# Attention feature map and MoE on one Trainium2 core: another staging of the MoE weights, issued by ScalarE, and other landing tiles for keys and queries

## The chip, the core and the metric

The kernel runs as one program on one core of a Trainium2 chip. The metric is the device time of one execution in microseconds (us). The kernel before was timed in three runs: 1204.83, 1207.55 and 1209.04 us, with the median at 1207.55 us. A fourth execution was recorded by the hardware profiler; all rows quoted here come from that one. The engines are called PE (matrix multiply), PEld (its weight loads), DVE (vector), ACT (scalar), POOL (GpSimd) and SP (the engine that here only issues DMAs).

## What is computed

Eight batches of eight heads with 576 tokens of 64 values go through an attention with a feature map, and the result through a two-layer MLP with 512, 2048 and 512 columns.

```python
def phi(x):
    proj = np.einsum('bhsd,df->bhsf', x, w_phi)
    proj = proj - np.max(np.abs(proj), axis=-1, keepdims=True)
    return np.concatenate([np.exp(proj), np.exp(-proj)], axis=-1)
q_p, k_p = phi(q), phi(k)
kv = np.einsum('bhsf,bhsd->bhfd', k_p, v)
z = np.sum(k_p, axis=2)
out = einsum('bhsf,bhfd->bhsd', q_p, kv) / (einsum('bhsf,bhf->bhs', q_p, z)[..., None] + 1e-06)
x = out as (4608 tokens, 512)
h = x @ w_in
return np.maximum(0.01 * h, h) @ w_out
```

The two weight matrices lie in HBM as 64-bit floats. The kernel brings each 128x512 piece of them in as 128x1024 32-bit words and rebuilds a 32-bit value from the halves of each pair on ACT and DVE. Then it splits that value into a high and a low part (names ending in h and l), because a matmul of the fast 32-bit type is taken three times: high by high, high by low, low by high.

## The kernel before: work, order and names

**Attention.** Two heads make a pair, so there are 32 pairs i, four to a batch. For each pair a key phase (`k_phase`) projects the keys (PE lines L405 or L244), takes the absolute maximum and the exponentials, and sums them against the values into one PSUM tile "c" (L224), which has a single buffer. A query phase (`q_phase`) projects the queries (L342 for pairs 4 to 7, L344 and L345 from pair 8 on). DVE transposes the result into the tile tq and reduces it (L346, L348). Three small DMAs gather the maxima over partitions (L350) and three spread them again (L355). Then DVE subtracts and transposes (L361, L363), ACT takes exponentials (L368, L369), DVE makes the high part (L375), and PE multiplies with the key sums (L384, L386, L389). Pairs 0 to 3 (batch 0) have versions of their own, the "first" phases (L405, L440, L517), which run with everything in tiles called f1 to f4. Pairs 0 to 7 use plain 32-bit matmuls, which show twice each in the profile.

**MLP.** Tokens go in 18 blocks of 256. A step (block, ft) has a first layer of 12 matmuls with 256 columns (L571, L572, L574), the activation (L578), the split, and a second layer of 6 matmuls with 512 columns (L591 to L593). Blocks 0 and 1 advance together through the 16 slices ft, and this is when the weights are staged; from block 2 on each block runs through all ft. The output of batch b stands in half b % 2 of the tile `ring` ("the x words"), and a block can only be split into xh and xl when the attention of all its tokens is there. Block 2 needs batch 1 (pairs 4 to 7), block 4 needs batch 2 (pairs 8 to 11), block 6 needs batch 3 (pairs 12 to 15).

**Weight staging** (`load_weights`). There are 32 pieces n = 0 to 31, the input weight and the output weight of each ft in turn. Each is a load (L169), an absolute value on ACT (L174), three DVE operations (L175 to L177), a second ACT operation (L179), a DVE addition (L180), a copy on ACT and a difference on DVE. The landing places before:

```python
if n < 10:    raw = two halves of ring[:, 1]
elif n < 24:  raw = (f4[:, 0:1024], f4[:, 1024:2048], f1[:, 0:1024])[n % 3]
else:         raw = qs tile if n % 2 else ring[:, 1, 2:4]
```

**What sets the order.** The program gives every operation a priority (front first, then attention, then staging, then the MLP), and a list scheduler with a cost model puts the instructions of each engine into one fixed order when the kernel is built. On the chip each engine runs its list in that order and waits at each instruction for what it needs. SP's list holds all DMAs before: loads of keys, values, queries and weights, the small DMAs of the query phase, and the output.

**Landing tiles before.** `load_k` (L191) lands the keys of pairs 5 and 7 in the tile `ks` and all others in `rk`; one buffer each. The values go into `rv` (L192 to L194), the queries into `rq` (L200). The third part of batch 0's queries (`first_load_q`, L470) also lands in `rq`.

Of the kernel before, what the change touches and what calls it, by code (L numbers as in the profile page):

```python
# [9 lines left out]
F32 = mybir.dt.float32  # L10
F32R = mybir.dt.float32r
I32 = mybir.dt.int32
U32 = mybir.dt.uint32
AF = mybir.ActivationFunctionType
# [30 lines left out]
def attention_moe_kernel(ctx: ExitStack, tc: tile.TileContext, q, k, v, vt, w_phi, w_in, w_out, out):  # L45
# [5 lines left out]
    def ct(shape, dt, name):  # L51
        return cp.tile(shape, dt, tag=name, name=name)

    def st(shape, dt, tag):
        return sp.tile(shape, dt, tag=tag, name=tag, bufs=BUFS.get(tag, 1))

    cnt = {}

# [5 lines left out]
    def copy_(key, o, i):  # L64
        e = pick(key) or "a"
        if e == "a":
            nc.scalar.copy(o, i)  # L67
        else:
            (nc.vector if e == "v" else nc.gpsimd).tensor_copy(o, i)  # L69

    def tt_(key, o, a, b, op):
        (nc.vector if pick(key) == "v" else nc.gpsimd).tensor_tensor(o, a, b, op=op)  # L72
# [8 lines left out]
    def weight(which, part, ft):  # L81
        g, f = divmod(ft, 4)
        if (which, part, g) not in weights:
            name = f"w{which}{part}{g}"
            weights[which, part, g] = (cp.tile([P, 4, DM], F32R, tag="late", name=name, bufs=4) if g == 3 else
                                       ct([P, 4, DM], F32R, name))
        return weights[which, part, g][:, f]
# [65 lines left out]
            nc.scalar.copy(wq_h[r], w)  # L153
            nc.vector.tensor_tensor(wq_l[r], w, wq_h[r].bitcast(F32), op=ALU.subtract)

    tail_stage = ring[:, 1, 2:4].rearrange("p a s -> p (a s)")

    def load_weights():
        n = 0
        for ft in range(NFT):  # L160
            for which, src in ((0, w_in), (1, w_out)):
                if n < 10:
                    raw = ring[:, 1, 2 * (n % 2) : 2 * (n % 2) + 2].rearrange("p a s -> p (a s)")[:, 0:1024]
                elif n < 24:
                    raw = (f4[:, 0:1024], f4[:, 1024:2048], f1[:, 0:1024])[n % 3]
                else:
                    raw = st([P, 2 * S], F32, "qs")[:, 0:1024] if n % 2 else tail_stage[:, 0:1024]
                raw = raw.bitcast(I32)
                nc.sync.dma_start(raw, src[:, ft].bitcast(I32))  # L169
                raw = raw.rearrange("p (n t) -> p n t", t=2)  # L170
                low, top = raw[:, :, 0], raw[:, :, 1]
                w = st([P, DM], F32, "ql")
                wi = w.bitcast(I32)
                nc.scalar.activation(w, top.bitcast(F32), AF.Abs)  # L174
                nc.vector.tensor_scalar(w, w, TINY, HUGE, op0=ALU.max, op1=ALU.min)  # L175
                nc.vector.tensor_scalar(wi, wi, 3, 0x3FFFFFF8, op0=ALU.logical_shift_left, op1=ALU.bitwise_and)
                nc.vector.scalar_tensor_tensor(wi, top, -0x40000000, wi, op0=ALU.bitwise_and, op1=ALU.bitwise_or)  # L177
                cr = st([P, DM], I32, "kvl")
                nc.scalar.activation(cr, low.bitcast(U32), AF.Copy, scale=2.0 ** -29)  # L179
                nc.vector.tensor_tensor(wi, wi, cr, op=ALU.add)  # L180
                h, l = weight(which, "h", ft), weight(which, "l", ft)
                copy_("h", h, w)
                tt_("l", l, w, h.bitcast(F32), ALU.subtract)
                n += 1

    kraw, qraw = {}, {}

    def load_k(i):
        rk = st([P, S], F32, "ks" if i < NK and i % 2 else "rk")
        rv = st([P, 10, 66], F32, "rv")  # L190
        nc.sync.dma_start(rk, k[i])  # L191
        nc.sync.dma_start(rv[:, 0:8, 0:64], v[i])  # L192
        nc.sync.dma_start(rv[0:64, 8:10, 0:64], vt[i])
        nc.sync.dma_start(rv[64:128, 8:10, 0:64], vt[i])  # L194
        nc.gpsimd.memset(rv[:, :, 64:66], 1.0)
        kraw[i] = rk, rv

    def load_q(i):
        rq = st([P, S], F32, "rq")
# [4 lines left out]

    def k_phase(i):
        nat = i < NK
        rk, rv = kraw.pop(i)
        if not nat:
            ks = st([P, 2, S], F32R, "ks")
            for j in range(2):  # L210
# [4 lines left out]
            copy_("vh", vh[:, :, 0:64], rv[:, :, 0:64])  # L215
            for r, c in ((slice(0, P), slice(0, 8)), (slice(64, P), slice(8, 10))):
                tt_("vl", vl[r, c], rv[r, c, 0:64], vh[r, c, 0:64].bitcast(F32), ALU.subtract)
        if i + 1 < B * NP:
            load_k(i + 1)
        yield  # L220
        kvp = pt("c")

# [4 lines left out]
        for g in range(3):  # L227
# [28 lines left out]
                nc.vector.tensor_scalar(m4n[r, 0 : 2 * w], m4[r, 0 : 2 * w], -1.0, None, op0=ALU.mult)  # L256
            if nat:
                nc.vector.tensor_tensor(pmk[r, 0 : 2 * w], pkv, mb, op=ALU.subtract)
            yield
            for s in range(w):  # L260
                c = 2 * g + s
# [24 lines left out]
                else:  # L286
# [3 lines left out]
                    for j in range(2):  # L290
                        kv_mm(j, vl[:, 8 + j], kst[:, j])
                        kv_mm(j, vh[:, 8 + j], kst[:, j], last=True)
                yield
        kvs = st([P, 2, 256], F32, "ek").rearrange("p a (b f) -> p a b f", b=2)[0:66]
        copy_("kvs", kvs, kvp[0:66].rearrange("p (a b f) -> p a b f", a=2, b=2))
        yield
# [114 lines left out]
    def first_k_phase(i):  # L411
        od = i % 2
        rk, rv = first_k.pop(i)
        if i == 2:
            load_k(NP)
        yield
        kvp = pt("h")
        for g in range(3):
# [43 lines left out]
    def first_load_q(u):  # L462
        t0, w = units[u]
        if u == 0:
            rq = st([P, NP, w], F32, "ks")
        elif u == 1:
            rq = part(f2, 0, [NP, w])
        else:
            rq = st([P, NP, w], F32, "rq")
        nc.sync.dma_start(rq, q[0:NP, :, t0 : t0 + w].rearrange("a p t -> p a t"))  # L470
        first_q[u] = rq

# [215 lines left out]
```

## Time and profile before

| | |
|---|---|
| median of three runs | 1207.55 us (1204.83 to 1209.04) |
| the profiled execution | 1207.22 us, of which the span of the trace is 1205.4 us |
| PE busy in the span | 1168.8 us, 97% |
| DVE, ACT, POOL busy | 747.7, 861.8, 631.5 us |
| matmul records | 7496 |
| weight loads of 512 KB | 28 in rows of ring and f tiles, 4 more in qs |

A row of the timeline gives start, duration, engine, line, operation, output and inputs, count, and in brackets the idle time before it with what ended it. A row of the windows gives a stretch, its length, and then the busy time and (number of instructions) of PE, PEld, DVE, ACT and POOL, the clock granted to PE as a share, the busy share of the DMA engines and GB/s. Ends of matmuls are modelled and overlap, so that the distance between starts is what a matmul costs. Lines are those of the kernel before unless said otherwise.

### The profile page before, as it was taken

To read this page: it belongs to the slowest core of one execution; us is meant where nothing else is said; L and a number is where in the kernel's file an instruction comes from. 1 tells how busy PE (TensorE), PEld (TensorE's weight loads), DVE (VectorE), ACT (ScalarE), POOL (GpSimd) and SP (SyncE) were. 2 spreads that over 40 slices of the span, in tenths; PEclk is the share of its full clock that TensorE was granted. 3 is DMA by queue.
4 is the path that set the end of the run, shared out by engine and by line. 5 is a ranking of instruction groups with operands and counts; after the bars stand their busy time and mean duration, and the time that the engine had idled before them with its cause. 6 is when DMAs were issued, how large, how long until landed. Compare 5 with 4: busy or idle time off the path is not lost.

```text
span 1205.4 us, 21633 instructions
## 1 busy us (share of the span) xinstructions
PE 1168.8 (97%) x7496; PEld 1035.9 (86%) x7496; DVE 747.7 (62%) x1327; ACT 861.8 (71%) x2267; POOL 631.5 (52%) x709
## 2 busy tenths in 40 slices
PE   8899999899998999899999999999999999999998
PEld 5577778699997999799998999899989999989997
DVE  5979984566767675766677666767876767510000
ACT  5977875778787787777787877778777788543232
POOL 0042222456566676666666666656566766453232
PEclk9999999899998999899999999999999999999999
DMA  7425241201111011111111011111011110000000
GB/s 215 142 81 167 88 116 32 77 23 33 50 32 48 18 44 33 50 24 32 50 32 40 22 50 33 40 33 50 21 40 32 41 33 19 3 18 5 14 18 18
DMA packets 70846, 57.82 MB, mean 48 GB/s; under 512 B 53201, under 2 KB 54353, under 8 KB 70737
## 3 DMA queue, kind: packets, MB, share of 16 engines
q1 hardware_dynamic: 70736, 56.44, 16.6%
q8 instruction: 59, 0.97, 0.3%
q14 instruction: 51, 0.41, 0.1%
HBM read 46.20 MB, written 9.44 MB: 46 GB/s over the span
## 4 chain that ended last, share of the span: by engine, by line
PE 69%; DVE 10%; ACT 9%; issue 4%; DMA 4%; SPq 2%; POOL 2%; DVEq 0%; POOLq 0%; ACTq 0%
PE h L571 9%; PE h L574 9%; PE h L572 9%; PE acc L591 8%; PE acc L592 8%; PE acc L593 8%; PE c L224 5%; PE a L384 2%; DMA mx<-mx 2%; PE a L244 2%; PE a L389 2%; PE a L386 2%; DMA m<-m 2%; DVE tq L361 1%; SPq L350 1%
## 5 line engine op out<-in xcount | busy, mean ns | idle before, releaser
L72 POOL TENSOR_TENSOR gl<-g,gh 128x256 fp32r<-128x256 f32 x288 | 231.3, 806 | 327.9 <-ACT gh L67 259.9
L571 PE MATMUL h<-xh,w0h 128*128 128x256 f32 x1088 | 281.1, 285 | 4.4 <-ACT g L578 2.4
L572 PE MATMUL h<-xh,w0l 128*128 128x256 f32 x1088 | 277.5, 282 | 0.0
L571 PEld LDWEIGHTS h<-xh,w0h 128*128 128x128 f32 x1088 | 205.9, 189 | 18.3 <-ACT g L578 4.2
L591 PE MATMUL acc<-w1h,gh 128*128 128x512 f32 x544 | 215.3, 396 | 0.7 <-DVE o L69 0.4
L592 PE MATMUL acc<-w1l,gh 128*128 128x512 f32 x544 | 214.8, 395 | 0.0
L572 PEld LDWEIGHTS h<-xh,w0l 128*128 128x128 f32 x1088 | 205.8, 189 | 8.9
L593 PE MATMUL acc<-w1h,gl 128*128 128x512 f32 x544 | 203.4, 395 | 0.7 <-POOL gl L72 0.7
L578 ACT ACTIVATE g<-h 128x256 f32<-128x256 f32 x288 | 109.1, 381 | 110.4 <-PE h L574 85.4
L574 PE MATMUL h<-xl,w0h 128*128 128x256 f32 x1088 | 187.4, 281 | 0.0
L72 POOL TENSOR_TENSOR ql<-eq,qh 128x576 fp32r<-128x576 f32 x96 | 148.8, 1569 | 53.6 <-DVE qh L375 31.7
L67 ACT CAST gh<-g 128x256 fp32r<-128x256 f32 x288 | 114.8, 403 | 57.5 <-PE acc L592 55.1
L574 PEld LDWEIGHTS h<-xl,w0h 128*128 128x128 f32 x1088 | 154.6, 188 | 0.6 <-POOL xl L72 0.2
L72 POOL TENSOR_TENSOR kpl<-ek,kph 128x512 fp32r<-128x512 f32 x72 | 98.4, 1366 | 37.4 <-ACT kph L67 14.5
L591 PEld LDWEIGHTS acc<-w1h,gh 128*128 128x128 f32 x544 | 102.4, 188 | 14.1 <-DVE o L69 0.7
L593 PEld LDWEIGHTS acc<-w1h,gl 128*128 128x128 f32 x544 | 99.1, 188 | 17.6 <-POOL gl L72 0.9
L592 PEld LDWEIGHTS acc<-w1l,gh 128*128 128x128 f32 x544 | 102.3, 188 | 12.6
L361 DVE TENSOR_TENSOR tq<-tq,mx 128x576 f32<-128x576 f32 x56 | 59.2, 1097 | 80.3 <-DMA mx<-mx 80.3
L269 ACT ACTIVATE ek<-pmk,m4n 128x128 f32<-128x128 f32 (+1 forms) x240 | 89.8, 393 | 16.1 <-POOL kpl L72 12.6
L375 DVE TENSOR_REDUCE qh<-eq 128x576 fp32r<-128x576 f32 x96 | 70.8, 749 | 44.4 <-ACT eq L369 20.2
L270 ACT ACTIVATE ek<-pmk,m 128x128 f32<-128x128 f32 (+1 forms) x240 | 89.1, 390 | 8.6 <-DVE m L252 8.1
L368 ACT ACTIVATE eq<-mb 128x288 f32<-128x288 f32 x112 | 49.2, 439 | 53.5 <-DVE mb L363 50.1
(202 smaller groups left out, 2363.9 us busy)
## 6 DMA issues: line engine op xcount, KB each, us to landing
out_dram<-o SPq DMA_DIRECT2D x35, 256.0 KB, 2.0
rq<-in_q_dram SPq DMA_DIRECT2D x28, 288.0 KB, 3.0
rk<-in_k_dram SPq DMA_DIRECT2D x27, 288.0 KB, 2.8
rv<-in_v_dram SPq DMA_DIRECT2D x29, 256.0 KB, 3.6
ring<-in_w_in_dram SPq DMA_DIRECT2D x9, 512.0 KB, 3.8
f<-in_w_out_dram SPq DMA_DIRECT2D x7, 512.0 KB, 3.6
f<-in_w_in_dram SPq DMA_DIRECT2D x7, 512.0 KB, 3.7
ring<-in_w_out_dram SPq DMA_DIRECT2D x5, 512.0 KB, 3.8
```

The lines of the kernel that those rows point to most:

```text
L67: nc.scalar.copy(o, i)
L72: (nc.vector if pick(key) == "v" else nc.gpsimd).tensor_tensor(o, a, b, op=op)
L269: nc.scalar.activation(ek[r, j, 0:F], pmk[r, h], AF.Exp, bias=m4n[r, h : h + 1])
L270: nc.scalar.activation(ek[r, j, F:256], pmk[r, h], AF.Exp, scale=-1.0, bias=m4[r, h : h + 1])
L361: nc.vector.tensor_tensor(tu, tu, mx[:, u].unsqueeze(2).broadcast_to([P, 18, 32]), op=ALU.subtract)
L571: nc.tensor.matmul(ph, lhsT=weight(0, "h", ft)[:, d * P : d * P + P], rhs=xh[d], start=d == 0, stop=False)
L572: nc.tensor.matmul(ph, lhsT=weight(0, "l", ft)[:, d * P : d * P + P], rhs=xh[d], start=False, stop=False)
L574: nc.tensor.matmul(ph, lhsT=weight(0, "h", ft)[:, d * P : d * P + P], rhs=xl[d], start=False, stop=d == NP - 1)
L578: nc.scalar.activation(g, ph, AF.Prelu, alpha=0.01)
L591: nc.tensor.matmul(a, lhsT=gh[:, ts], rhs=weight(1, "h", ft), start=ft == 0, stop=False)
L592: nc.tensor.matmul(a, lhsT=gh[:, ts], rhs=weight(1, "l", ft), start=False, stop=False)
L593: nc.tensor.matmul(a, lhsT=gl[:, ts], rhs=weight(1, "h", ft), start=False, stop=ft == NFT - 1)
```

## The change

The pieces 10 to 23 land in eight half tiles (f3, f4, f1, f2, two halves each) in place of three, up to four pieces ahead of the staging, and their 14 loads are issued by ACT instead of SP. The pieces 24 to 31 alternate between the tiles `ks` and `qs`, so the x words of batch 1 are no longer used by them. Since `ks` is taken, keys always land in `rk`: for pairs up to 7 the next keys are loaded when the last projection of the present pair has been read, and the next values after its last product. The third part of batch 0's queries lands in f3.

```diff
+    halves = [f[:, o : o + 1024] for f in (f3, f4, f1, f2) for o in (0, 1024)]
+    def load_weight(n):
+        if n < 10:
+            raw = ring[:, 1, 2 * (n % 2) : 2 * (n % 2) + 2].rearrange("p a s -> p (a s)")[:, 0:1024]
+        elif n < 24:
+            raw = halves[(n - 10) % 8]
+        else:
+            raw = st([P, 2, S], F32, "qs" if n % 2 else "ks", "raw").rearrange("p a s -> p (a s)")[:, 0:1024]
+        raws[n] = raw = raw.bitcast(I32)
+        (nc.scalar if 10 <= n < 24 else nc.sync).dma_start(raw, (w_in, w_out)[n % 2][:, n // 2].bitcast(I32))
...
+        for n in range(2 * NFT):
+            for m in range(len(raws), 2 * NFT):
+                if m > n + (1 if m < 10 or m >= 24 else 4):
+                    break
+                load_weight(m)
...
     def load_k(i):
-        rk = st([P, S], F32, "ks" if i < NK and i % 2 else "rk")
+        rk = st([P, S], F32, "rk")
...
-        if i + 1 < B * NP:
+        if not nat and i + 1 < B * NP:
             load_k(i + 1)
+            load_v(i + 1)
...
             if nat:
                 nc.vector.tensor_tensor(pmk[r, 0 : 2 * w], pkv, mb, op=ALU.subtract)
+                if g == 2:
+                    load_k(i + 1)
...
+        if nat:
+            load_v(i + 1)
...
-            rq = st([P, NP, w], F32, "rq")
+            rq = part(f3, 512, [NP, w])
```

No operation on PE, DVE or POOL is added or taken away, but the scheduler orders all engines anew. Three places matter for what follows.

The first is PE at the keys of pair 5, near the end of batch 0's own phases. Here rk_203 holds the keys of pair 4, and ks_1020 (before) or rk_1064 (after) those of pair 5. Before:

```order
L405 MATMUL a_1064<-bd_73,rk_203 128x256
L517 MATMUL c_549<-qs_546,f3_82 128x256 x2
L571 MATMUL h_1506<-qh_74,w0h0_638 128x256
L572 MATMUL h_1506<-qh_74,w0l0_639 128x256
L405 MATMUL a_1095<-bd_73,ks_1020 128x256 x2
```

After:

```order
L418 MATMUL a_1060<-bd_73,rk_203 128x256
L531 MATMUL c_548<-qs_545,f3_82 128x256 x2
L585 MATMUL h_1509<-qh_75,w0h0_638 128x256
L586 MATMUL h_1509<-qh_75,w0l0_639 128x256
L418 MATMUL a_1091<-bd_73,rk_1064 128x256 x2
```

The distance in PE's list between the last projection of pair 4 and the first of pair 5 is the same, but the keys of pair 5 now land in the one buffer of rk, which the first row still reads.

The second place is ACT at the end of batch 0's phases. The rows "ring<-c" and "dn<-c" empty PSUM tile "c" for its last unit of tokens. Before:

```order
L520 COPY ring<-c 64x4x64
L521 ACTIVATE dn<-c 64x256
L67 CAST qh<-ring 128x256
L520 COPY ring<-c 64x4x64
L521 ACTIVATE dn<-c 64x256
L578 ACTIVATE g<-h 128x256
L67 CAST gh<-g 128x256
```

After:

```order
L534 COPY ring<-c 64x4x64
L535 ACTIVATE dn<-c 64x256
L592 ACTIVATE g<-h 128x256
L167 DMA f_81<-in_w_out_dram 128x1024
L167 DMA f_80<-in_w_out_dram 128x1024
L167 DMA f_83<-in_w_out_dram 128x1024
L534 COPY ring<-c 64x4x64
L535 ACTIVATE dn<-c 64x256
L167 DMA f_82<-in_w_in_dram 128x1024
L67 CAST gh<-g 128x256
```

Four of the 14 loads now stand here in ACT's list; four stand earlier, in batch 0's phases, and six later.

The third place is PE behind the last query projection of pair 11 (the "qs,wq" rows), where it fills the time until the attention product of that pair (L384 before, L397 after). Before, from that projection on:

```order
L345 MATMUL a<-qs,wq 128x288
L244 MATMUL a<-wq,ks 128x256 x2
L574 MATMUL h<-xl,w0h_914 128x256
L591 MATMUL acc<-w1h_835,gh 128x512
L592 MATMUL acc<-w1l_836,gh 128x512
L593 MATMUL acc<-w1h_835,gl 128x512
L591 MATMUL acc<-w1h_835,gh 128x512
L244 MATMUL a<-wq,ks 128x256 x2
L592 MATMUL acc<-w1l_836,gh 128x512
L593 MATMUL acc<-w1h_835,gl 128x512
L571 MATMUL h<-xh,w0h_914 128x256
```

After:

```order
L358 MATMUL a<-qs,wq 128x288
L253 MATMUL a<-wq,ks 128x256 x2
L588 MATMUL h<-xl,w0h_916 128x256 x4
L605 MATMUL acc<-w1h_930,gh 128x512
L606 MATMUL acc<-w1l_931,gh 128x512
L607 MATMUL acc<-w1h_930,gl 128x512
L605 MATMUL acc<-w1h_930,gh 128x512
L606 MATMUL acc<-w1l_931,gh 128x512
L607 MATMUL acc<-w1h_930,gl 128x512
L585 MATMUL h<-xh,w0h_638 128x256
L586 MATMUL h<-xh,w0l_639 128x256
```

After the change the second layer of the slice before (w1h_835) and eight first-layer matmuls have moved ahead of the projection, and the next block's first layer (w0h_638) stands there sooner. Counted up to the attention product, before has 25 first-layer, 30 second-layer, 4 key-projection and 12 key-sum matmuls; after has 16, 24, 4 and 12. Behind the last query projection of pair 15 the same counts are 24, 27, 4 and 12 (and 4 transposes) before, and 18, 24, 4 and 12 (and 4 transposes) after. Behind that of pair 7 nothing has changed: 30, 18, 4 and 10 in both.

On DVE, the operations of batch 0's phases stand earlier against the staging: the ninth maximum of its query part (L487 before) has 104 DVE instructions ahead of it before and 95 after, and the addition L180 of piece 9 has 105 and 113. At the end of these phases the counts are equal again. On ACT, the last exponential of its query part has 120 before it before, and 126 after, four of them DMAs.

More of the change, by code (lines that the diff above doesn't have):

```diff
@@ L52, in ct, with st @@
         return cp.tile(shape, dt, tag=name, name=name)
-    def st(shape, dt, tag):
-        return sp.tile(shape, dt, tag=tag, name=tag, bufs=BUFS.get(tag, 1))
+    def st(shape, dt, tag, name=None):
+        return sp.tile(shape, dt, tag=tag, name=name or tag, bufs=BUFS.get(tag, 1))
     cnt = {}
@@ L154, in split_w_phi @@
             nc.vector.tensor_tensor(wq_l[r], w, wq_h[r].bitcast(F32), op=ALU.subtract)
-    tail_stage = ring[:, 1, 2:4].rearrange("p a s -> p (a s)")
-    def load_weights():
[L159 to L184, printed above, removed]
@@ L186, in attention_moe_kernel @@
-    kraw, qraw = {}, {}
+    halves = [f[:, o : o + 1024] for f in (f3, f4, f1, f2) for o in (0, 1024)]
+    raws = {}
+    def load_weight(n):
[7 more added lines that the diff above has]
+        (nc.scalar if 10 <= n < 24 else nc.sync).dma_start(raw, (w_in, w_out)[n % 2][:, n // 2].bitcast(I32))
@@ new lines, in load_weights @@
+    def load_weights():
+        for n in range(2 * NFT):
+            which, ft = n % 2, n // 2
+            for m in range(len(raws), 2 * NFT):
+                if m > n + (1 if m < 10 or m >= 24 else 4):
+                    break
+                load_weight(m)
+            raw = raws[n].rearrange("p (n t) -> p n t", t=2)
+            low, top = raw[:, :, 0], raw[:, :, 1]
+            w = st([P, DM], F32, "ql")
+            wi = w.bitcast(I32)
+            nc.scalar.activation(w, top.bitcast(F32), AF.Abs)
+            nc.vector.tensor_scalar(w, w, TINY, HUGE, op0=ALU.max, op1=ALU.min)
+            nc.vector.tensor_scalar(wi, wi, 3, 0x3FFFFFF8, op0=ALU.logical_shift_left, op1=ALU.bitwise_and)
+            nc.vector.scalar_tensor_tensor(wi, top, -0x40000000, wi, op0=ALU.bitwise_and, op1=ALU.bitwise_or)
+            cr = st([P, DM], I32, "kvl")
+            nc.scalar.activation(cr, low.bitcast(U32), AF.Copy, scale=2.0 ** -29)
+            nc.vector.tensor_tensor(wi, wi, cr, op=ALU.add)
+            h, l = weight(which, "h", ft), weight(which, "l", ft)
+            copy_("h", h, w)
+            tt_("l", l, w, h.bitcast(F32), ALU.subtract)
@@ L188, in load_k, with load_v @@
+    kraw, vraw, qraw = {}, {}, {}
     def load_k(i):
-        rk = st([P, S], F32, "ks" if i < NK and i % 2 else "rk")
+        rk = st([P, S], F32, "rk")
+        nc.sync.dma_start(rk, k[i])
+        kraw[i] = rk
+    def load_v(i):
         rv = st([P, 10, 66], F32, "rv")
-        nc.sync.dma_start(rk, k[i])
         nc.sync.dma_start(rv[:, 0:8, 0:64], v[i])
@@ L195, in load_k @@
         nc.gpsimd.memset(rv[:, :, 64:66], 1.0)
-        kraw[i] = rk, rv
+        vraw[i] = rv
     def load_q(i):
@@ L206, in k_phase @@
         nat = i < NK
-        rk, rv = kraw.pop(i)
+        rk, rv = kraw.pop(i), vraw.pop(i)
         if not nat:
@@ L415, in first_k_phase @@
             load_k(NP)
+            load_v(NP)
         yield
```

## Prediction

> **What bounds the kernel now.** I began with the page's head:
>
> ```profile
> span 1205.4 us, 21633 instructions
> PE 1168.8 (97%) x7496; PEld 1035.9 (86%) x7496; DVE 747.7 (62%) x1327; ACT 861.8 (71%) x2267; POOL 631.5 (52%) x709
> ```
>
> PE is the bound, and the change leaves all its matmuls as they are. So only the stretches count in which PE stands idle or runs at a lower clock. The table by windows finds them:
>
> ```profile
> 20.00:37.00 17.00, 16.68 (x79) 10.45 (x78) 15.24 (x29) 14.56 (x31) 0.12 (x1) 1.00 0.63 183
> 37.00:61.00 24.00, 19.59 (x99) 14.34 (x98) 21.45 (x45) 23.35 (x53) 3.02 (x4) 1.00 0.47 143
> 61.00:75.00 14.00, 12.94 (x64) 10.04 (x63) 12.93 (x26) 12.02 (x30) 6.54 (x8) 1.00 0.18 59
> 75.00:87.00 12.00, 11.10 (x70) 9.00 (x68) 5.69 (x14) 6.89 (x21) 5.49 (x8) 1.00 0.38 113
> 87.00:220.00 133.00, 131.48 (x728) 102.53 (x727) 103.59 (x191) 98.91 (x237) 34.14 (x46) 1.00 0.33 94
> 226.00:240.00 14.00, 9.89 (x39) 6.96 (x38) 7.14 (x12) 10.74 (x28) 3.31 (x3) 0.76 0.42 133
> 363.00:378.00 15.00, 10.94 (x55) 9.45 (x54) 11.91 (x23) 12.46 (x33) 10.54 (x8) 0.77 0.17 55
> 498.00:514.00 16.00, 10.70 (x55) 9.51 (x54) 14.27 (x23) 12.24 (x31) 9.73 (x8) 0.79 0.15 51
> 1100.00:1160.00 60.00, 60.00 (x382) 54.20 (x381) 0.69 (x1) 20.26 (x53) 21.65 (x30) 1.00 0.03 11
> ```
>
> Batch 0's phases, 20 to 87 us, leave PE idle for 0.3, 4.4, 1.1 and 0.9 us; ACT is full from 37 to 61 (23.35 of 24) and DVE from 61 to 75 (12.93 of 14). The staging stretch, 87 to 220, leaves 1.5 us. Three short stretches, where blocks 2, 4 and 6 wait for the attention of pairs 7, 11 and 15, leave 4.1, 4.1 and 5.3 us at a granted clock of 0.76 to 0.79. The last row is PE undisturbed: 382 matmuls in 60 us are 0.157 us each, so a step of 18 takes 2.83 us; with the 512-column ones counted double, a first-layer matmul costs 0.118 and a second-layer one 0.236 us.
>
> **Staging itself: no gain.** The last difference of the staging, the first use of the last slice, and a row of the DMA view with a load's time to landing:
>
> ```profile
> 184.72 0.69 DVE L72 TENSOR_TENSOR w1l<-ql,w1h 128x512 fp32r<-128x512 f32 x1
> 215.95 0.38 PE L571 MATMUL h<-xh,w0h 128*128 128x256 f32 x1
> f<-in_w_in_dram SPq DMA_DIRECT2D x7, 512.0 KB, 3.7
> ```
>
> The weights are ready 215.95 - 185.41 = 30.5 us early. Loads that come up to four pieces ahead are hidden by this cover: 0. If it were gone, each piece would show a load's 3.7 us to landing. The x words, which the last pieces give up, bring 0 as well: PE's list reaches pair 7 at the same place as before, with the same 62 matmuls behind its last projection.
>
> **The keys of pair 5.** Before they wait in ks; after they can be loaded only when pair 4's last projection has been read. The load that used that very moment before is pair 6's:
>
> ```profile
> 75.68 0.59 PE L405 MATMUL a<-bd,rk 128*128 128x256 f32 x2
> 76.30 0.33 SPq L191 DMA_DIRECT2D rk<-in_k_dram  x1
> 77.88 1.10 PE L405 MATMUL a<-bd,ks 128*128 128x256 f32 x4 [0.17 <-issue]
> 81.57 2.00 PE L517 MATMUL c<-eq,f 128*128 128x64 f32 x16 [0.57 <-ACT dn L521]
> rk<-in_k_dram SPq DMA_DIRECT2D x6, 288.0 KB, 3.0
> ```
>
> 76.30 + 3.0 = 79.3, and PE, with the same four matmuls between, is there at 77.88: a new wait of 1.4 us at a row behind which all of PE's list queues. The 0.57 us before the products at 81.57 can shrink in return. Bounds 0.8 and 1.5; I take +1.1. For pairs 6 and 7 PE's list has over 20 us of work in between, counted at the prices above, so nothing is late there.
>
> **The loads on ACT.** SP waited a long time at weight loads, and no row shows a load issued by ACT:
>
> ```profile
> SPq L169 <- DVE ql L177: 63.2, 20, 6.5
> 68.77 0.33 SPq L169 DMA_DIRECT2D ring<-in_w_in_dram  x1
> ```
>
> An issue takes SP 0.33 us where nothing stands before it. The bounds for ACT are 0 (the issue runs while the operation before is still executing) and 0.33 us. Of the 14, four stand where ACT is full: 0 to 1.3 us. I take 0.5, nearer to nothing, because PE there also waits for DVE. Four stand at the end of these phases, three of them behind operands that PE frees one by one in the same eight products that ACT must wait for anyway (the row at 81.57): 0, up to 1.0 if they come only behind the last. Six stand in the staging stretch, where ACT is idle for 133 - 98.9 = 34 us and PE needs its results a step (2.83 us) later: 0. What queues behind a waiting load on ACT is the activation and split of the next steps, and PE waits for those; that is a rival below.
>
> SP loses 14 loads and their waits. Its small DMAs for the query phases may go out sooner, but between 87 and 220 us PE has only 1.5 us to win, most of it in these:
>
> ```profile
> PE h L571 <- ACT g L578: 0.8, 2, 0.6
> PE a L384 <- ACT eq L368: 0.7, 1, 0.7
> ```
>
> I count -0.7, bounds -1.5 and +1.
>
> The Trainium skill, "DMA: Bandwidth & Descriptors", section "Issuing engines are not separate DMA queues", says that starting transfers from several engines saves only the sequencer's time of issue. By that rule the sum would hold nothing here for faster landing; the trace so far agrees, since a 512 KB load took 3.7 us whatever stood ahead of it on SP.
>
> **The order within batch 0's phases.** DVE reaches the ninth maximum nine instructions sooner; at 12.93 / 26 = 0.50 us each that is up to 4.5 us less where DVE is full. ACT reaches the last exponential two operations later (without the DMAs), at 23.35 / 53 = 0.44 us each 0.9 us more where ACT is full. PE waits there mostly for ACT:
>
> ```profile
> PE h L571 <- ACT xh L67: 1.8, 2, 1.2
> PE h L517 <- ACT dn L521: 1.6, 4, 0.6
> PE c L517 <- ACT dn L521: 1.0, 2, 0.6
> ```
>
> All the staging of pieces 0 to 9 still comes before the end of these phases, so the work of both engines up to there is the same. I take -0.5, bounds -4.5 and +2.
>
> **Pairs 11 and 15: less work to cover the query chain.** From the last query projection to the first attention product a chain runs through DVE, two rounds of DMAs, DVE and ACT:
>
> ```profile
> 229.07 0.81 PE L384 MATMUL a<-eq,kvh 128*128 128x288 f32 x2 [2.47 <-ACT eq L368]
> 351.60 0.38 PE L345 MATMUL a<-qs,wq 128*128 128x288 f32 x1
> 366.30 0.61 PE L384 MATMUL a<-qh,kvh 128*128 128x288 f32 x1 [1.36 <-DVE qh L375]
> 487.29 0.29 PE L345 MATMUL a<-qs,wq 128*128 128x288 f32 x1
> 502.87 0.61 PE L384 MATMUL a<-qh,kvh 128*128 128x288 f32 x1 [3.54 <-DVE qh L375]
> ```
>
> It takes 14.70 us for pair 11 and 15.58 for pair 15 (the first row is pair 7's product), and PE ends by waiting for DVE's last step, so the chain sets the time, not PE. PE's list after holds less work there. For pair 11 nine first-layer and six second-layer matmuls are gone: 9 x 0.118 + 6 x 0.236 = 2.5 us. For pair 15 six and three: 1.4 us. That work is done ahead of the projection, where PE is busy anyway, so each wait grows by as much. I take +2.4 and +1.4; the bounds are 0 each (the chain shrinks with a later start) and the full amounts plus 1.7 us each, half of what the clock of 0.77 took from 363 to 378 (15 x 0.23 = 3.45). For pair 7 the lists agree: 0. The other pairs from 8 on have some 14 us or more of cover in both lists, counted at the same prices, against a chain of about 15: I leave them at 0, ±1.5 for all together.
>
> On that clock: it was 0.77 in 363 to 378, where PE was idle for 4.1 us in all and 1.36 us at a stretch before the product. The Trainium skill, "TensorE: Matmul & The Clock Gate", section "Why this matters for your kernels", asks for no idle gap over some 3 us between bursts, since one idle window brings the half clock back. By that rule a longer wait costs pair 11 a further window of half clock, an estimate of 1.7 us from the page's 3.4 us window; the trace disagrees in so far as shorter gaps had already brought it, so the sum holds nothing for it.
>
> **The sum**, against the profiled execution's 1207.2 us (0.3 us under the median of the three runs): loads on ACT +0.5, staging stretch -0.7, keys of pair 5 +1.1, order in batch 0's phases -0.5, pair 11 +2.4, pair 15 +1.4. That is +4.2, so 1211.4 us: slower by 0.32% of the median, at the edge of the 0.3% (3.6 us, so 1203.9 to 1211.2) that a measurement of this kernel can tell from no change.
>
> **Rivals.**
>
> Not slower: batch 0's phases get shorter. DVE's nine instructions come off the path that ends at 75 us: -4.5 in place of -0.5, so 1211.4 - 4.0 = 1207.4; if pairs 11 and 15 then also wait no more than before, 1203.6. For it: DVE is full from 61 to 75. Against it: PE's waits there name ACT, and ACT is full just before. It decides from where PE's idle time in 20 to 87 us, now 6.7 us, falls under some 3.
>
> Nothing moves: the query chain of pairs 11 and 15 starts later on PE but shortens by as much, and the rest cancels. 1211.4 - 3.8 = 1207.6. For it: the chain's length differs among the two pairs by 0.9 us already. Against it: its DMA rounds and DVE steps are the same. The skill's rule on issuing engines, quoted above, gives this too: moved issues and nothing else, 1207.2.
>
> ACT blocked: a load in ACT's list waits for a buffer that DVE frees, as SP did for 63.2 / 20 = 3.2 us on average. Ten of the 14 reuse a tile; if the last six wait so long on ACT, that is 19 us in a stretch of some 40 us in which ACT has 34 x 40 / 133 = 10 us idle, so PE falls behind by up to 9: 1220. For it: everything behind the load waits. Against it: the scheduler put each load behind ACT's own reading of the tile it reuses, and other ACT operations of the staging wait for DVE there in any case. The Trainium skill, "PSUM — Partial Sum Buffer", section "Engine vs sequencer instructions", calls ScalarE's queue strictly first in, first out; by that rule nothing could pass the waiting load.
>
> **Chances and range.** The forecast's case has 0.5, batch 0's phases shorter 0.25, nothing moves 0.15, ACT blocked 0.1. The forecast's own range is 1207.5 to 1215 and straddles the edge, so I count 0.28 of it as slower and 0.22 as the same. The second case gives 0.15 faster and 0.10 the same, the third 0.12 the same and 0.03 faster, the fourth slower. So: faster 0.18, same 0.44, slower 0.38. The range reaches down into the second case and up to the upper bounds of the ACT and clock terms: 1204 to 1217.5.
>
> **What would show it.** Right: PE's list waits about 1.4 us at the first projection of pair 5 for its keys; 75 to 220 us keep their length otherwise; the waits before the first products of pairs 11 and 15 grow by 2.4 and 1.4 us; pair 7's stays at 2.47. Wrong: idle time of PE before 87 us under 3 us; ACT rows that wait for a DVE release behind a load, with PE waiting for the activation (L592 of the changed kernel) or its cast; a query chain of pair 11 well under 14.7 us; or new waits in blocks 8 and later, which this sum holds at nothing.

## The result, and the profile of the changed kernel

The changed kernel takes 1213.76 us (median of five executions, 1212.75 to 1216.06) against 1209.04 us for the kernel before (five, 1204.83 to 1209.60): a ratio of 1.0051, 95% interval 1.0033 to 1.0069. It is slower. The forecast was 1211.4 us, with a range from 1204 to 1217.5. The profiled executions, 1212.84 and 1207.22 us, are 5.6 us apart, as their spans are.

The head of the changed kernel's page:

```profile
span 1211.0 us, 21600 instructions
PE 1165.4 (96%) x7496; PEld 1034.2 (85%) x7496; DVE 752.7 (62%) x1327; ACT 863.5 (71%) x2267; POOL 633.2 (52%) x709
```

PE still does its 7496 matmuls and is still the bound. Its table by windows, the stretches that the prediction showed of before (length, PE, PEld, DVE, ACT and POOL busy, PE's granted clock, DMA share, GB/s):

```profile
20.00:37.00 17.00, 17.00 (x84) 10.98 (x83) 14.93 (x28) 13.68 (x29) 0.26 (x1) 1.00 0.64 182
37.00:61.00 24.00, 18.14 (x96) 13.74 (x94) 21.56 (x46) 22.67 (x51) 3.39 (x5) 1.00 0.53 170
61.00:75.00 14.00, 11.45 (x55) 8.71 (x55) 13.04 (x27) 11.93 (x29) 6.89 (x9) 1.00 0.17 56
75.00:87.00 12.00, 10.36 (x71) 9.11 (x70) 4.70 (x11) 7.12 (x20) 3.44 (x5) 1.00 0.35 89
87.00:220.00 133.00, 131.87 (x730) 103.18 (x730) 105.76 (x195) 100.72 (x240) 35.24 (x47) 1.00 0.31 91
226.00:240.00 14.00, 8.81 (x38) 6.54 (x38) 8.04 (x12) 11.25 (x29) 3.76 (x4) 0.88 0.40 132
363.00:378.00 15.00, 8.66 (x39) 7.18 (x38) 11.68 (x18) 10.61 (x28) 8.36 (x7) 0.77 0.17 55
498.00:514.00 16.00, 10.77 (x51) 8.23 (x49) 11.68 (x15) 11.30 (x30) 10.36 (x8) 0.79 0.17 55
```

From 20 to 87 us PE is idle for 0 + 5.9 + 2.5 + 1.6 = 10.0 us, where it was 6.7. That is not where the time went, though. A busy share can't say that, since the two lists hold their work in another order; places with the same work ahead of them can. The first products of pairs 7, 11 and 15 are such places: in both traces 1120, 1992 and 2864 matmul records of the same kinds stand ahead of them. Rows of the changed kernel's timeline: the first product of pair 7, and those of pairs 11 and 15, each with the last query projection that leads to it:

```profile
228.91 0.75 PE L397 MATMUL a<-eq,kvh 128*128 128x288 f32 x2 [2.47 <-ACT eq L381]
...
353.81 0.29 PE L358 MATMUL a<-qs,wq 128*128 128x288 f32 x1
...
367.52 0.46 PE L397 MATMUL a<-qh,kvh 128*128 128x288 f32 x1 [3.75 <-DVE qh L388]
...
492.11 0.30 PE L358 MATMUL a<-qs,wq 128*128 128x288 f32 x1
...
507.49 0.61 PE L397 MATMUL a<-qh,kvh 128*128 128x288 f32 x1 [2.69 <-DVE qh L388]
```

Before, the products began at 229.07, 366.30 and 502.87 us. So the changed kernel is 0.16 us ahead at pair 7's product, 1.2 us behind at pair 11's, 4.6 us behind at pair 15's and 5.6 us behind at the end. All that lies ahead of 229 us, the staging, the loads on ScalarE, the landing tiles and 3.3 us of added idle time, comes to nothing; 1.4 us come before pair 11's product, 3.4 between the two products, 1.0 after.

### The profile page after: what moved, and what is told of

Read it like the earlier page. It is cut to its first block, busy times and chain, and to the rows that moved or that the text cites. A ratio compares the mean times of both kernels' runs of the same rounds, so it can differ in the third digit from the quotient of the medians.

```text
span 1211.0 us, 21600 instructions
## 1 busy us (share of the span) xinstructions
PE 1165.4 (96%) x7496; PEld 1034.2 (85%) x7496; DVE 752.7 (62%) x1327; ACT 863.5 (71%) x2267; POOL 633.2 (52%) x709
## 3 DMA queue, kind: packets, MB, share of 16 engines
q1 hardware_dynamic: 68720, 49.10, 14.7%
## 4 chain that ended last, share of the span: by engine, by line
PE 67%; DVE 11%; ACT 10%; DMA 4%; issue 4%; SPq 3%; POOL 1%; DVEq 0%; ACTq 0%; POOLq 0%
PE h L585 9%; PE h L588 9%; PE h L586 9%; PE acc L605 8%; PE acc L607 8%; PE acc L606 8%; PE c L233 5%; PE a L397 2%; PE a L253 2%; PE a L399 2%; PE a L402 2%; DMA mx<-mx 1%; DMA m<-m 1%; DVE tq L374 1%; PE a L357 1%
## 5 line engine op out<-in xcount | busy, mean ns | idle before, releaser
L585 PEld LDWEIGHTS h<-xh,w0h 128*128 128x128 f32 x1088 | 206.1, 189 | 15.9 <-ACT g L592 3.1
L588 PE MATMUL h<-xl,w0h 128*128 128x256 f32 x1088 | 184.6, 282 | 0.0
L374 DVE TENSOR_TENSOR tq<-tq,mx 128x576 f32<-128x576 f32 x56 | 53.9, 1000 | 56.6 <-DMA mx<-mx 56.5
L72 POOL TENSOR_TENSOR ring<-ring,dn 128x288 f32<-128x288 f32 x56 | 48.7, 869 | 66.7 <-DVE dn L412 43.7
```

The costliest lines, as they stand in the source:

```text
L585: nc.tensor.matmul(ph, lhsT=weight(0, "h", ft)[:, d * P : d * P + P], rhs=xh[d], start=d == 0, stop=False)
L588: nc.tensor.matmul(ph, lhsT=weight(0, "h", ft)[:, d * P : d * P + P], rhs=xl[d], start=False, stop=d == NP - 1)
```

## The experiments

Three theories stood against each other. "Order": the change moves PE's list, less work stands behind the last query projections of pairs 11 and 15, and so PE waits longer for the query chain. "Staging": the loads on ScalarE or their landing cost the time. "Later order": the list behind 511 us does. In these texts, cover is the work in PE's list between the last query projection of a pair and its first product, priced as in the prediction (0.118 us for a matmul of 256 columns, 0.236 for one of 512). It is 9.4, 11.9 and 11.1 us for pairs 7, 11 and 15 before, and 9.4, 9.4 and 9.7 in the changed kernel; the recorded expectations count 0.1 to 0.2 us less for the same lists. The executions of the kernel before beside the runs had medians of 1208.12 (first four), 1208.49 (next four) and 1208.40 us (last four); the ratios are to those.

**Halves alone.** The changed kernel with three of its edits taken back (here the main lines):

```diff
-        rk = st([P, S], F32, "rk")
+        rk = st([P, S], F32, "ks" if i < NK and i % 2 else "rk")
...
-            raw = st([P, 2, S], F32, "qs" if n % 2 else "ks", "raw")...
+            raw = st([P, 2 * S], F32, "qs")[:, 0:1024] if n % 2 else ring[:, 1, 2:4]...
...
-            rq = part(f3, 512, [NP, w])
+            rq = st([P, NP, w], F32, "rq")
```

> Only the staging of the changed kernel: eight halves, fourteen loads issued by ScalarE; keys, last steps and the query tile of the last unit as in the kernel before. Theory 'order' (the loss is the shorter cover behind the last query projections of pairs 11 and 15): PE's list from 219 us on is that of the kernel before, with 25 first- and 30 second-layer matmuls behind pair 11's last query projection and 24 and 27 behind pair 15's, so those waits are as before (1.4 and 3.5 us) and the keys of pair 5 are there in time: 1209, between 1207.5 and 1210. Rival 'staging' (the loads on ScalarE, their issue or their landing, cost the time): 1212 to 1214, with the loss in 37 to 220 us.

Measured: 1209.07 us, ratio 1.0008 (0.9996 to 1.0019). The first products of pairs 11 and 15 in its timeline:

```profile
366.94 0.40 PE L393 MATMUL a<-qh,kvh 128*128 128x288 f32 x1 [1.36 <-DVE qh L384]
...
504.40 0.61 PE L393 MATMUL a<-qh,kvh 128*128 128x288 f32 x1 [2.88 <-DVE qh L384]
```

The wait at pair 11 is again the 1.36 us of before, and that at pair 15 is 2.88 us (3.54 before), though the fourteen loads are on ScalarE. The rival "staging" is out: eight halves and loads on ScalarE cost nothing that this measurement can tell.

**Keys alone.** The kernel before with the key landing tiles only:

```diff
-        rk = st([P, S], F32, "ks" if i < NK and i % 2 else "rk")
+        rk = st([P, S], F32, "rk")
...
+                if g == 2:
+                    load_k(i + 1)
```

> Only the key landing tiles of the changed kernel, staging as before, all loads on SyncE. PE's list is that of the kernel before up to pair 15 in all that matters (25 and 30 behind pair 11's last query projection), but pair 15 has 12 first- and 22 second-layer matmuls instead of 24 and 27, and from 511 us on the list is that of the changed kernel. Theory 'order': a wait of 1 us at pair 5's first projection, pair 11 as before, pair 15 later by 12 x 0.118 + 5 x 0.236 = 2.6 us: 1212.6, between 1211.5 and 1214. Rival 'staging': 1209 to 1210. Rival 'later order' (the loss comes from the list behind 511 us): some 1211 even if pair 15's wait does not grow.

Measured: 1212.86 us, ratio 1.0041 (1.0025 to 1.0056).

```profile
365.77 0.40 PE L392 MATMUL a<-qh,kvh 128*128 128x288 f32 x1 [1.36 <-DVE qh L383]
...
506.30 0.61 PE L392 MATMUL a<-qh,kvh 128*128 128x288 f32 x1 [4.08 <-DVE qh L383]
```

Pair 11's product waits as before and comes no later (366.30 before); pair 15's comes 3.4 us later. Most of the loss is there, made by an edit that moves the loads of keys and values, with the staging untouched. Since pair 15 loses as its cover foretells, the rival "later order" is not needed for it; what lies behind pair 15's product is 1.7 us (a span of 1210.6 us against 1205.4). One detail missed: the wait of 1 us at pair 5 did not come, since in this list other work stands between the load of the keys and the projection.

**Query tile alone.** The kernel before with the third edit:

```diff
-            rq = st([P, NP, w], F32, "rq")
+            rq = part(f3, 512, [NP, w])
```

> The kernel before with the third edit alone: the query tile of batch 0's last unit in a free part of f3. Cover behind the last query projection: pairs 7 and 11 as before, pair 15 9.3 us (16 first- and 24 second-layer matmuls) instead of 11.0 (24 and 27). Theory 'order': 1.7 us slower than before from pair 15 alone, up to twice that with the half clock: 1208.5 + 1.7 = 1210.2, between 1209 and 1212. Rival (a tile that only lands elsewhere changes nothing): 1208.5.

Measured: 1211.60 us, ratio 1.0023 (1.0013 to 1.0033): slower, at the upper part of the range. In its profile pair 15 waits 4.20 us, and pair 11's product waits 3.11 us with its cover unchanged, because its chain took 15.9 us instead of 14.7; the last section shows in which step. But this profiled execution is the slowest of the twelve (1213.69 us), and it reaches pair 7's last query projection at 219.51 us, where the kernel before is there at 215.62: 3.9 us of its loss lie in the front part, away from the cover, and their cause is open. So this run shows the sign that the order theory forecast, but not how much of the time is the cover's.

**All loads issued by SyncE.**

```diff
-        (nc.scalar if 10 <= n < 24 else nc.sync).dma_start(raw, ...)
+        nc.sync.dma_start(raw, ...)
```

> The changed kernel with all loads issued by SyncE. The list moves too: behind pair 7's last query projection stand 18 and 12 matmuls (30 and 18 in the changed kernel), behind pair 11's 30 and 30 (16 and 24), behind pair 15's 24 and 29 (18 and 24). Theory 'order': pair 7 waits 1.8 us more, pair 11 waits 3.0 less and pair 15 1.9 less than in the changed kernel: 1213.8 - 3.1 = 1210.7, between 1209 and 1212, with no gain in 20 to 87 us. Rival 'staging': the stretch from 20 to 87 us gets shorter by 2 us or more.

Measured: 1211.89 us (1.0034, 1.0018 to 1.0049). The first products of pairs 7, 11 and 15:

```profile
232.37 1.17 PE L397 MATMUL a<-eq,kvh 128*128 128x288 f32 x2
...
369.11 0.40 PE L397 MATMUL a<-qh,kvh 128*128 128x288 f32 x1 [1.97 <-DVE qh L388]
...
505.36 0.40 PE L397 MATMUL a<-qh,kvh 128*128 128x288 f32 x1 [1.12 <-DVE qh L388]
```

Pairs 11 and 15 wait 1.97 and 1.12 us, less than the changed kernel's 3.75 and 2.69, as the cover says; pair 7's product begins 3.5 us later than there, where 1.8 were expected. PE's idle time from 20 to 87 us is 8.0 us instead of 10.0, but measured by the work done PE is 0.5 us later at 214 us than in the changed kernel: nothing is gained ahead of pair 7's product by taking the issues from ScalarE.

**Last steps in the x words again.**

```diff
-            raw = st([P, 2, S], F32, "qs" if n % 2 else "ks", "raw")...
+            raw = st([P, 2 * S], F32, "qs")[:, 0:1024] if n % 2 else ring[:, 1, 2:4]...
```

> The changed kernel with the even pieces of the last steps in the x words again. PE's list is the changed kernel's but for 15 matmuls between 80 and 186 us. Theory 'order': 1213.8, between 1213 and 1215, with pair 7's, 11's and 15's waits as in the changed kernel. If the x words mattered, pair 7's products would come later: its wait of 2.5 us grows by 1 us or more, and the time with it.

Measured: 1213.78 us (1.0045, 1.0029 to 1.0060), the changed kernel's time to 0.02 us. Where the last steps land is worth nothing that this measurement can tell.

**Without the DMA rounds.** This kernel leaves work out: for pairs 7, 11 and 15 the maxima are not combined over the four groups of rows. In q_phase of the changed kernel:

```diff
+        edge = i in (7, 11, 15)
-        for a in range(1, 4):
+        for a in range(1, 1 if edge else 4):
             nc.sync.dma_start(m[0:32, a], m[32 * a : 32 * a + 32, 0])
...
+        if edge:
+            nc.vector.tensor_copy(mx, m[:, 0])
...
-        for a in range(1, 4):
+        for a in range(1, 1 if edge else 4):
             nc.sync.dma_start(mx[32 * a : 32 * a + 32], mx[0:32])
```

> The changed kernel without the two rounds of DMAs in the query chains of pairs 7, 11 and 15 (their maxima are not combined over the four groups of rows; a copy stands in place). In the changed kernel the two rounds take 7 us of the chain (355.96 to 363.02 us for pair 11). Cover behind the last query projection falls too, from 9.3, 9.3 and 9.6 us to 6.0, 7.5 and 7.9. Theory 'chain' (the length of the query chain less the cover is what PE waits for): the chains get 6 to 7 us shorter, 7 to 9 us, so the waits of 2.7, 3.9 and 4.6 us between last projection and first product fall to about 1 each; 9 us less and some of the half clock: 1204, between 1200 and 1206.5. Rival (the waits belong to something else in those stretches, the value loads or VectorE's work for the next pair's keys): 1211 or more.

Measured: 1201.34 us (0.9933, 0.9921 to 0.9945), 12.4 us under the changed kernel. Its first products of pairs 11 and 15:

```profile
358.97 0.29 PE L401 MATMUL a<-qh,kvh 128*128 128x288 f32 x1
...
495.41 0.29 PE L401 MATMUL a<-qh,kvh 128*128 128x288 f32 x1
```

No wait stands at these rows any more, and PE's idle time from last projection to first product falls from 3.9 and 4.6 us to 1.0 and 0.9. So it is the query chain, with its DMA rounds, that PE waits for in these stretches, and not another step there.

**Two issuers.** One of the three DMAs of a round goes to ScalarE, in the changed kernel and in the halves-alone kernel:

```diff
-            nc.sync.dma_start(m[0:32, a], m[32 * a : 32 * a + 32, 0])
+            (nc.scalar if a == 2 and i in EDGE else nc.sync).dma_start(m[0:32, a], m[32 * a : 32 * a + 32, 0])
```

> The changed kernel with one of the three DMAs of each round in the query chains of pairs 7, 11 and 15 issued by ScalarE instead of SyncE; nothing left out. Three on SyncE took 1.84 us to issue, 0.61 each. Cover: pair 7 as in the changed kernel, pair 11 9.6 us (9.3), pair 15 11.5 (9.6). Theory 'chain': 0.6 us less for each round, 1.2 for each of three chains, 3.6 in all, and 2.2 from the cover: 1208, between 1206 and 1210. Rival (landing, not issue, sets a round): only the cover's 2.2: 1211.6.

> The halves-alone kernel (1209.1) with one of the three DMAs of each round in the query chains of pairs 7, 11 and 15 issued by ScalarE. Cover: pairs 7 and 11 as in that kernel, pair 15 9.3 us instead of 11.0. Theory 'chain': -3.6 for the rounds, +1.7 for pair 15's cover: 1207.2, between 1205.5 and 1209. Rival (landing, not issue, sets a round): 1210.8.

Measured: 1208.06 us (0.9994, 0.9985 to 1.0004) and 1210.49 us (1.0019, 1.0010 to 1.0028). The first hits its number, the second misses by 3.3 us and comes to what the rival on record, landing, had for it (1210.8); for the first that rival had 1211.6. The profile shows that the step behind both was wrong in part. Pair 11's two rounds in the halves-alone kernel, with the maximum between them and the subtraction behind (SPq and ACTq are DMA issues):

```profile
354.61 1.84 SPq L359 DMA_DIRECT2D m<-m  x3
...
357.67 0.41 DVE L362 TENSOR_REDUCE mx<-m 32x36 f32<-32x144 f32 x1 [1.23 <-DMA m<-m]
358.11 2.36 SPq L364 DMA_DIRECT2D mx<-mx  x3
361.75 2.19 DVE L370 TENSOR_TENSOR tq<-tq,mx 128x576 f32<-128x576 f32 x2 [3.68 <-DMA mx<-mx]
```

and with two issuers:

```profile
356.73 1.45 SPq L360 DMA_DIRECT2D m<-m  x2
356.73 0.53 ACTq L360 DMA_DIRECT2D m<-m  x1
...
359.40 0.41 DVE L363 TENSOR_REDUCE mx<-m 32x36 f32<-32x144 f32 x1 [0.84 <-DMA m<-m]
359.83 1.15 SPq L365 DMA_DIRECT2D mx<-mx  x2
359.84 0.52 ACTq L365 DMA_DIRECT2D mx<-mx  x1
364.01 2.07 DVE L371 TENSOR_TENSOR tq<-tq,mx 128x576 f32<-128x576 f32 x2 [4.20 <-DMA mx<-mx]
```

The issue is shorter in both rounds, but the first lands 0.4 us sooner (2.67 us from issue to the maximum instead of 3.06) and the second 0.5 us later (4.18 instead of 3.64). Over three pairs the chains are 0.3, 0.2 and 1.4 us shorter, not 1.2 each; in the other kernel they are 0.7 us shorter, 0.3 longer and 1.4 shorter. Landing sets most of a round. The 1208.06 us then rest on pair 15's cover (11.6 us instead of 9.7) and on its chain (13.97 us instead of 15.38) more than on the reason given. The second kernel's profiled execution, 1212.46 us, is also 3.2 us late at pair 7's last projection (218.85 us), as the query-tile kernel was; that part has nothing to do with the chains of pairs 11 and 15.

**Keys and last steps as before.** The changed kernel with its landing tiles and its last steps taken back, the query tile kept:

> The changed kernel with its key landing tiles and its last steps as before: eight halves, loads on ScalarE and the query tile of the last unit stay. From 219 us on PE's list is that of the keys-alone kernel, which differs from it only by the staging. Theory 'order': the time of the keys-alone kernel, 1212.9, between 1211.5 and 1214, though neither the staging nor the landing tiles are the same; pair 15 waits as there. If staging or landing tiles had a price of their own, it would be 1 us or more away from that.

Measured: 1214.70 us (1.0050, 1.0036 to 1.0063), 0.7 us outside what was expected. The interval overlaps that of the keys-alone kernel, so a price of 1 to 2 us for halves and query tile together is neither shown nor excluded. Pair 15 waits 4.07 us, as there. But the way to the time is another one: at pair 7's last projection this kernel is 4.1 us behind the keys-alone kernel (219.23 us against 215.12), and at the end only 0.9 us (spans of 1211.5 and 1210.6 us). So the closeness of the two times does not confirm the theory. In the front part its profile has clock lost at a place where, of the others, only the query-tile kernel has any (0.90):

```profile
75.00:87.00 12.00, 10.59 (x58) 9.24 (x57) 4.96 (x12) 6.21 (x19) 3.07 (x5) 0.82 0.53 157
```

**Another way to the maxima.** If the chain of three pairs is what costs, a shorter chain should make the kernels alike, and faster. In q_phase of the changed kernel, of the halves-alone kernel and of the kernel before, for pairs 7, 11 and 15 only:

```diff
+            pk = pt("a")
+            for j in range(2):
+                nc.tensor.matmul(pk[r, 256 * j : 256 * j + 256], lhsT=qs[:, j, t], rhs=wq..., start=True, stop=True)
...
+            nc.vector.tensor_reduce(m4, y, axis=AX.X, op=ALU.max, apply_absolute_value=True)
+            nc.vector.tensor_tensor(x, y, mq, op=ALU.subtract)
...
+                    for s in range(3):
+                        nc.tensor.transpose(mj[:, s * P : s * P + n], slots[3 * u + s][0:n, j], ident[0:n, 0:n])
```

> The changed kernel with another way to the query maxima of pairs 7, 11 and 15, nothing left out: the projection puts tokens on the rows, so a maximum runs along a row on VectorE, and TensorE turns the result round (twelve transposes a pair) in place of VectorE's block transposes and the two rounds of DMAs. Added work of PE, from the changed kernel's rows: twelve projection matmuls of 0.20 us for eight of 0.13 (pairs 11 and 15, 1.3 us each), twelve transposes of some 0.1 us (1.2 each): 6 us in all. Theory 'chain': the chains fall from 13.5 to 15.4 us to about 6, the waits of 2.7, 3.9 and 4.6 us and the half clock go as they did without the rounds (12.4 us less): 1213.8 - 12.4 + 6 = 1207.4, between 1204 and 1209. Rival (PE's added work eats all of it): 1213 or more.

> The same query phases of pairs 7, 11 and 15 in the halves-alone kernel. Theory 'chain': if the cover behind the last query projections of pairs 11 and 15 was all that made the changed kernel slower than this one, the two should come to the same time once their chains are short: 1207, between 1204 and 1209, within 1.5 us of the changed kernel with this edit, where they were 4.7 us apart. Rival (the 4.7 us lie elsewhere): this one stays 4 to 5 us ahead.

> The same query phases of pairs 7, 11 and 15 in the kernel before. Theory 'chain': within 1.5 us of the other two with this edit, so 1207, between 1204 and 1209: the staging, the landing tiles and the loads on ScalarE are then worth nothing either way. Rival: as far ahead of the changed kernel with this edit as the kernel before is of the changed one (4.7 us).

Measured: 1205.49 us (0.9973, 0.9956 to 0.9990), 1205.05 us (0.9968, 0.9957 to 0.9978) and 1204.18 us (0.9961, 0.9947 to 0.9975). The three are within 1.3 us of each other, where the changed kernel stood 4.7 and 5.4 us behind the other two; all three beat both kernels. The first products of pairs 11 and 15, in the changed kernel with this edit and in the kernel before with it:

```profile
364.64 0.29 PE L436 MATMUL a<-qh,kvh 128*128 128x288 f32 x1
...
499.89 0.40 PE L436 MATMUL a<-qh,kvh 128*128 128x288 f32 x1 [0.57 <-DVE qh L427]
```

```profile
362.41 0.29 PE L423 MATMUL a<-qh,kvh 128*128 128x288 f32 x1
...
496.37 0.29 PE L423 MATMUL a<-qh,kvh 128*128 128x288 f32 x1
```

PE's busy time has grown (1170.7 us instead of 1165.4 in the changed kernel), and the waits have shrunk by more.

## Why the prediction was right

The sign was the one forecast, though the chances had "the same" (0.44) ahead of "slower" (0.38). The main mechanism, less cover and longer waits in front of pairs 11 and 15, was right too, but it gave only part of the time, and the sum came near with some luck: it was 1.4 us short in the profiled execution (+4.2 against +5.6). By its steps:

**Staging, loads on ScalarE, front, keys of pair 5: +0.4, came to -0.2.** Their parts did not come as priced. The wait for pair 5's keys is there:

```profile
77.32 0.33 SPq L195 DMA_DIRECT2D rk<-in_k_dram  x1
...
80.20 1.10 PE L418 MATMUL a<-bd,rk 128*128 128x256 f32 x4 [0.98 <-DMA rk<-in_k_dram]
```

0.98 us, inside the bounds of 0.8 and 1.5. The front was forecast 0.5 us better; in its place PE's idle time there grew by 3.3 us, the keys' 1.0 among them. That this vanished by 229 us was not foreseen in that form: the list holds its work in another order, and pair 7's last query projection starts no later (215.45 us, 215.62 before). That four terms of either sign and their measured parts both come to about nothing is luck. On ScalarE the loads found room:

```profile
84.58 1.30 ACTq L167 DMA_DIRECT2D f<-in_w_out_dram  x3
85.92 0.37 ACT L534 COPY ring<-c 64x256 f32<-64x256 f32 x1 [1.68 <-PE c L531]
```

Three in a row took 1.30 us, inside 1.68 us in which ScalarE waited for PE anyway. Of the fourteen, three went out ahead of 37 us and one only between 37 and 61, where I had counted four. The rival "ACT blocked" (1220) is out by the halves-alone kernel, the rival "batch 0's phases get shorter" by the 10.0 us of idle time.

**Pair 7: 0.** Its wait is 2.47 us in both.

**Pair 11: +2.4, came to 1.4 ahead of the product and about 2 behind it.** The wait at the product grew by 3.75 - 1.36 = 2.4 us, the number forecast. But the chain also shortened, from 14.70 to 367.52 - 353.81 = 13.71 us (0.5 of it in VectorE's two subtractions, 1.54 us instead of 2.02), which the prediction had named as a sign against it, and a wait of 0.84 us just ahead of the product before went. So PE's idle time from projection to product grew by 1.65 us (2.20 to 3.85) and not by 2.4, and the product came only 1.4 us later against pair 7's: part of the rival "nothing moves" was in it, as the lower bound allowed. That the wait at the product hit its number is luck. What the shorter chain gave back was lost again behind the product, in idle time and at a lower clock. The 24 us from the product on, in the changed kernel, in the kernel before, and in the one with its last steps in the x words, whose product waits as long as the changed kernel's:

```profile
367.00:379.00 12.00, 8.98 (x39) 7.99 (x40) 8.24 (x12) 9.87 (x26) 8.09 (x6) 0.67 0.15 46
379.00:391.00 12.00, 11.91 (x83) 11.22 (x82) 10.30 (x19) 7.71 (x20) 5.31 (x7) 0.90 0.01 2
```

```profile
366.00:378.00 12.00, 9.84 (x50) 9.07 (x51) 9.01 (x17) 11.14 (x30) 9.10 (x7) 0.72 0.21 69
378.00:390.00 12.00, 11.91 (x89) 11.04 (x88) 9.23 (x19) 8.30 (x22) 6.43 (x8) 1.00 0.10 28
```

```profile
368.45 0.61 PE L397 MATMUL a<-qh,kvh 128*128 128x288 f32 x1 [3.75 <-DVE qh L388]
```

```profile
366.00:378.00 12.00, 7.50 (x34) 6.36 (x34) 8.89 (x14) 10.12 (x27) 7.98 (x6) 0.72 0.15 46
378.00:390.00 12.00, 11.25 (x85) 10.16 (x85) 10.58 (x21) 8.36 (x21) 4.93 (x7) 1.00 0.01 2
```

In the changed kernel PE is idle there for 3.1 us instead of 2.2, and the missing clock is 12 x 0.33 + 12 x 0.10 = 5.2 us of full speed instead of 12 x 0.28 = 3.4. The sum had held this at nothing and the bounds at +1.7 us. The Trainium skill, "TensorE: Matmul & The Clock Gate", section "Why this matters for your kernels", would have added a further window of half clock for a longer gap, and the changed kernel's trace alone looks like it. The third kernel's trace does not: its gap is the same 3.75 us and its missing clock 12 x 0.28 = 3.4 us, as before (its first window begins ahead of the product, so that all of it is counted). Measured by the work done, pair 11 costs it 2.3 us (from 0.7 us behind the kernel before at 350 us to 3.0 at 385), where it costs the changed kernel 3.5. So what the changed kernel lost at the lower clock does not follow from its longer wait, and what decides it is open. Nor does the clock carry the whole difference: behind pair 7's product 14 x 0.12 = 1.7 us are missing (226 to 240 us) where 14 x 0.24 = 3.4 were, and over the whole trace, by its records of the granted clock, it is 10.3 us against 10.2.

**Pair 15: +1.4, came to 1.2 ahead and about 1.4 behind.** The chain of 507.49 - 492.11 = 15.38 us stayed (15.58 before). The wait at the product itself fell, 2.69 us instead of 3.54, where the prediction had it grow by 1.4; but another of 1.54 us, for GpSimd, stands just ahead of it, and PE's idle time from projection to product is 4.58 us instead of 3.63. Between the products of pairs 11 and 15 lie 3.4 us: about 1.2 of this wait and the 2 behind pair 11. Behind 507 us lies 1.0.

**All other pairs: 0 ± 1.5.** From pair 15's product to the end the loss is 1.0 us, and pair 15's own products take it: PE is idle for 4.1 us in the 24 us from there on, instead of 2.0. With the two executions laid against each other by the work that PE has done (its matmuls in the order of the list, each at its price), the changed kernel is 0.4 us ahead from 253 to 354 us, 3.2 to 3.4 behind from 383 to 484, 6.0 behind at 534, between 5 and 9 behind later, where the two lists hold the same work in another order, and 5.2 at PE's last matmul: -0.8 for blocks 8 and later, inside the bounds.

So the mis-sized term is the one for pairs 11 and 15: 3.8 us were forecast, and 6.4 measured up to 534 us (from 0.4 ahead to 6.0 behind). The waits that the sum was about, from the last projection to the first product, grew by 1.65 + 0.95 = 2.6 us, less than forecast; the rest is idle time and clock behind the first products, which the sum held at nothing. The experiments carry the attribution to the order of PE's list: equal cover, equal time (halves alone); a shorter cover at pair 15 by another edit, the loss at pair 15 (keys alone); short chains, no difference between the orders that the measurement can tell (the three kernels with rows). The query-tile run gives the sign alone. How a longer wait turns into lost time behind the product is not shown.

## What to carry to other kernels

Where a scheduler writes the order, an edit is priced first by what its new order leaves behind the starts of the long chains: count the work between the step that starts a chain and the step that needs its end, and compare it with the chain's length. In this kernel edits as small as the place where a tile lands moved that by 1.7 us (query tile) and 2.6 us (keys), and the kernel by 0.2 and 0.4%, though in the first part of the loss lies elsewhere. If such waits stand in the profile, shorten the chain; here that made three different orders alike, and faster by 3 to 4 us than the kernel before. And compare more than one profile before a lower clock is put down to a longer wait.

## What the runs showed of the hardware

**The same gap does not always bring the lower clock.** The changed kernel and the one with its last steps in the x words have the same wait at the same place, and only the second shows a lower clock behind it (at pair 11's product, above, the first shows more of it). The row and the window of each, the changed kernel first:

```profile
61.25 0.70 PE L531 MATMUL c<-eq,f 128*128 128x256 f32 x2 [2.08 <-ACT dn L535]
```

```profile
60.00:75.00 15.00, 11.45 (x55) 8.71 (x55) 14.04 (x30) 12.91 (x31) 7.36 (x9) 1.00 0.20 66
```

```profile
61.19 0.70 PE L531 MATMUL c<-eq,f 128*128 128x256 f32 x2 [2.09 <-ACT dn L535]
```

```profile
60.00:75.00 15.00, 12.40 (x51) 9.44 (x52) 14.03 (x29) 12.79 (x30) 6.81 (x8) 0.89 0.31 99
```

0.11 x 15 = 1.7 us of clock are there in one and not in the other. Executions of one kernel differ by more than that (1206.29 to 1210.90 us for the kernel before, beside the second four); whether the clock is the reason was not tested.

**VectorE's subtraction takes up to two and a half times as long beside GpSimd.** Pair 11's two subtractions, 128x576 each, and the GpSimd operation that ends as they begin or lies beside them, in the changed kernel, in the kernel before and in the query-tile kernel:

```profile
361.98 1.30 POOL L72 TENSOR_TENSOR kpl<-ek,kph 128x512 fp32r<-128x512 f32 x1 [0.71 <-ACT kph L67]
...
363.02 1.54 DVE L374 TENSOR_TENSOR tq<-tq,mx 128x576 f32<-128x576 f32 x2 [0.45 <-DMA mx<-mx]
```

```profile
361.29 2.02 DVE L361 TENSOR_TENSOR tq<-tq,mx 128x576 f32<-128x576 f32 x2 [3.87 <-DMA mx<-mx]
...
362.65 1.78 POOL L72 TENSOR_TENSOR kpl<-ek,kph 128x512 fp32r<-128x512 f32 x1
```

```profile
365.52 3.12 DVE L361 TENSOR_TENSOR tq<-tq,mx 128x576 f32<-128x576 f32 x2 [3.98 <-DMA mx<-mx]
...
366.21 1.82 POOL L72 TENSOR_TENSOR kpl<-ek,kph 128x512 fp32r<-128x512 f32 x1
```

1.54 us where GpSimd's operation ends as they begin, 2.02 and 3.12 where GpSimd is at work beside them: 1.1 of the 1.2 us by which the query-tile kernel's chain is longer than that of before. The changed kernel has 56 such subtractions in all: the 17 with no GpSimd operation beside them took 0.75 to 0.76 us each, the 36 with one beside them for more than 0.1 us took 0.75 to 1.90. The Trainium skill, "SBUF — State Buffer", section "SBUF: two separate sides", says that such a VectorE operation with two inputs in SBUF and a GpSimd operation hold the port pair they share for a whole instruction, and the other one blocks; these rows agree. No run took GpSimd's part away, so this cause is argued from the rows and not tested.
